# Retention feeding two MLPs: the first sweep's second token block runs inside the first block's sweep, with attention packed one chunk to a step

## The chip, the cores and the metric

One NeuronCore of a Trainium2 chip runs the whole kernel. The metric is the device time of one execution in microseconds (us), as the median of several runs. TensorE (PE) does the matmuls, VectorE (DVE), ScalarE (ACT) and GpSimd (POOL) do elementwise work, and SyncE (SP) issues most of the DMA transfers; ACT issues some too.

## The reference

```python
for t in range(768):            # 4 batches, 8 heads, head size 64
    state = gamma * state + k[t]^T v[t]
    y[t] = scale * q[t] @ state
x = y as 3072 tokens x 512
h = x @ w_in;  x = (h * cos(h)) @ w_out          # first MLP, 512 -> 2048 -> 512
h = x @ w_in2
g = h if h >= 1; 0 if h <= -1; else (h + 1)**2 / 4
out = g @ w_out2                                 # second MLP, same sizes
```

## The kernel before, in words

The retention is done by chunks of 128 positions: for chunk `n` PE makes the scores (`scores`, line 327), DVE multiplies them with a decay mask (`masks`, 339), PE adds scores times v and decayed q times the state (`attend`, 379 and 385), ACT and DVE split the result into a rounded part and a rest (`finish`, 117 and 399), PE makes k times v (`kv`, 350) and DVE puts it into the state of its batch (`update`, 365 and 367). POOL decays q and k (`decay_q` 315, `decay_k` 305). Chunk `n` belongs to position group `n // 4`; the state that chunk `n` reads is updated by chunk `n - 4`. Four chunks make one block of 512 tokens, so there are six blocks.

The first MLP has 16 slices of 128 hidden columns ("chunks" of the hidden size, `j`). A sweep `k = 0` runs all six blocks over the first eight, a sweep `k = 1` runs them over the other eight; the partial output of the first sweep is stored in `yp_d` and added in the second. A pair (block, slice) is a step. In step `i` PE does `first` (12 matmuls of 512 columns, line 435) and then `second` of step `i - 3` (12 matmuls, line 500), since activation and splitting of a step take that long. `act` puts the work of a step on ACT and DVE in a fixed order: h to integer part (448), product of the step before (476) and its rounding (477), remainder (452), absolute value (455), rest (480), sine (459), then the callbacks in `mid`, then the weight conversion. With the last slice of a block `evacuate` copies four PSUM banks out.

Weights come as 64-bit floats and have to be converted. A conversion passes through `Conveyor` in stages, one for each call of `advance`: load (SP, 143, into one of three `raw` buffers), one step later `one` (DVE, 150 and 154) and `two` (ACT, 159 and 160), then `three` (DVE, 165 and 169) and `four` (POOL, 175), then `five` (ACT rounds, 117: `wih` or `woh`) and `six` (POOL subtracts, 120: `wil` or `wol`). A matmul of slice `j` needs `wih`/`wil` for `first` and `woh`/`wol` three steps later. The first five conversions (w_in 0, 1, 2, w_out 0, w_in 3) are started ahead of step 0. Of the sweep's 16 weight tiles, 11 are left for steps 0 to 6.

Blocks come one after the other: steps 0 to 7 are block 0, 8 to 15 block 1. Ahead of step 0 stand the four chunks of block 0. The four chunks of the next block are spread over the eight steps of a block, scores in an even step and attend in the odd one. The order of each engine is the order in which the program writes it (a manual schedule); each engine runs its own list in order, and waits where an operand is not there yet.

Of the kernel before, what the change touches and what calls it, by code (L numbers as in the profile page):

```python
# [11 lines left out]
F32 = mybir.dt.float32  # L12
# [9 lines left out]
P = 128  # L22
# [18 lines left out]
def tile_retention_mlp_mlp(  # L41
# [21 lines left out]
    CB = TB // C  # L63
    LAG = 3
    NWARM = 10

# [3 lines left out]
    yT_d = [dram.tile([P, NP, TB], F32, name=f"yT{j}") for j in range(NB)]  # L70
    yp_d = [dram.tile([P, NP, TB], F32, name=f"yp{j}") for j in range(NB)]
    w32_d = {
        (m, j, a): dram.tile([P, TB], F32, name=f"w32_{m}_{j}_{a}")
# [178 lines left out]
    class Attention:  # L252
# [17 lines left out]
        def load_mask(self):  # L270
            nc.sync.dma_start(out=self.mask_sb, in_=mask.rearrange("p (r c t) -> p r c t", r=2, c=NP))

# [16 lines left out]
        def load_v(self, n):  # L289
            if n >= NCH:  # L290
                return
            self.v[n] = self.ap.tile([P, NP, P], F32, tag="v", name="v", bufs=5)
            nc.sync.dma_start(out=self.v[n], in_=v[n].rearrange("p (c s) -> p c s", c=NP))

# [112 lines left out]

    JS = (range(NH), range(NH, NF))
# [13 lines left out]
    def load_part(b):  # L422

        t = xt[1, b][0].bitcast(F32)
        nc.sync.dma_start(out=t, in_=yp_d[b])
        for e in range(NP):
            part[b, e] = t[:, e, :]

# [11 lines left out]

    def act(k, b, j, done=(), fill=(), mid=()):
# [25 lines left out]

# [17 lines left out]
    def second(i):  # L485
        k, b, j = steps[i]
        gh, gl = gs.pop((k, b, j))
        wh, wl = wt[0, j, 1]
        begin, last = j == JS[k][0], j == JS[k][-1]
        if begin:  # L490
            acc[k, b] = [bank(e) for e in range(NP)]
        parts = ((wh, gh), (wl, gh), (wh, gl))
        if last:
# [3 lines left out]
        for e, i in order:  # L497
            s = slice(e * P, (e + 1) * P)
            w, g = parts[i]
# [4 lines left out]
        return [(k, b, e) for e in range(NP)] if last else ()  # L504

    def evacuate(done, n):
        for k, b, e in itertools.islice(done, n):
            a = acc[k, b][e]
            o = tp.tile([P, TB], F32, tag="r", name="o", bufs=5)
            if e % 2 == 0 and k == 1:  # L510
                nc.vector.tensor_tensor(out=o, in0=a, in1=part.pop((b, e)), op=ALU.add)
            elif e % 2 == 0:
                nc.vector.tensor_copy(out=o, in_=a)
            else:
                nc.scalar.activation(out=o, in_=a, func=AF.Copy)
                if k == 1:
                    nc.gpsimd.tensor_tensor(out=o, in0=o, in1=part.pop((b, e)), op=ALU.add)
            nc.sync.dma_start(out=(yp_d, yT_d)[k][b][:, e, :], in_=o)

# [307 lines left out]
    def run():  # L827
        i = 0
        with ExitStack() as es:
            att = Attention(es)  # L830
            stage = es.enter_context(tc.tile_pool(name="stage", bufs=1, reuse_waits="tile"))

            order = sorted([(j + a * LAG, 1 - a, j, a) for j in range(NH) for a in range(2)])
            todo = [Convert(0, j, a, True) for _, _, j, a in order]
            todo += [Convert(0, j, a, False) for j in range(NH, NF) for a in range(2)]

            att.load_t(0)
            att.load_mask()
# [4 lines left out]
            att.load_t(2)  # L843
            att.load_v(2)
            att.load_t(3)
            att.load_v(3)

# [5 lines left out]

            att.scores(0, (4, 5))
            att.masks(0)
            att.scores(1, (6, 7))
            att.masks(1)
            for n in range(CB):
                att.attend(n, 2 + n % 2)
                att.finish(n)  # L860
                if n + 2 < CB:
                    att.scores(n + 2, (4, 5) if n % 2 == 0 else (6, 7))
                    att.masks(n + 2)
                if n != 2:
                    conv.step(todo.pop(0), stage)
                if n == 0:
                    att.load_kdec()
                    att.load_k(0)
                    att.load_t(CB)
            att.load_qdec(1)  # L870
            for n in range(1, CB):
                att.load_k(n)
            att.decay_k(0)
            conv.step(todo.pop(0), stage)
            att.load_v(CB)
            att.load_k(CB)
            att.load_t(CB + 1)
            att.decay_q(CB)
            for n in range(1, CB + 1):
                att.decay_k(n)  # L880
            count = iter((1, 1, 2, 2, 2, 2, 1))
            for b in range(NB - 1):
                for l in range(NH):
                    n = (b + 1) * CB + l // 2
                    now = next(count, 0) if b == 0 else (b == 1 or l % 2) and bool(todo)
                    conv.start(todo.pop(0) if now else None, stage)
                    first(*steps[i], 4 + i % 2)
                    if l % 2 == 0:
                        att.load_t(n + 2)
                        att.load_v(n + 1)  # L890
                        att.load_k(n + 1)
                        if l == 2:
                            att.load_qdec(b + 2)
                        att.scores(n, (6, 7))
                        mid = [lambda: att.masks(n)]
                        if i == 0:
                            att.kv(0, 0)
                            mid.append(lambda: att.update(0))
                    else:
                        att.decay_q(n + 1)  # L900
                        att.decay_k(n + 1)
                        att.attend(n, 7)
                        att.kv(n, 6)
                        mid = [lambda: att.finish(n), lambda: att.update(n)]
                        if i == 1:
                            for m in range(1, CB):
                                att.kv(m, m)
                                mid.append(lambda m=m: att.update(m))
                    done = second(i - LAG) if i >= LAG else ()
                    act(*steps[i], done, mid=mid)  # L910
                    if now == 2:
                        conv.step(todo.pop(0), stage)
                    i += 1
            assert not todo
# [3 lines left out]
        with ExitStack() as es:  # L918
# [6 lines left out]
            while i < len(steps):  # L925
                k, b, j = steps[i]
                l = j - JS[k][0]
                fill = []
# [3 lines left out]
                n = blocks.index((k, b)) + 1  # L932
                late = l - len(JS[k]) + NH
                if k == 1 and l == NH - 1:
# [13 lines left out]
                act(k, b, j, done, fill)  # L948
                if n < len(blocks) and late == LAG - 1:
                    load_parts(blocks[n][1])  # L950
# [76 lines left out]
```

## Time and profile before

| | |
|---|---|
| median of 3 runs | 1156.74 us (1156.09 to 1157.53) |
| the profiled execution | 1156.66 us |
| its span, first to last instruction | 1154.9 us |
| PE busy | 1122.9 us, 97% of the span |
| DVE, ACT, POOL busy | 781.2, 725.0, 470.1 us |
| granted TensorE clock, mean | 0.985 of full |

Some 1.8 us of the execution lie outside the span. A clock of 1.00 is 2.4 GHz; the lower level, 1.2 GHz, shows as 0.5. A matmul of 512 columns that follows another starts some 0.23 us after it at the higher level and some 0.43 us at the lower. PE's busy time counts slow matmuls as busy, so idle time and clock are read together.

### The profile page before, as it was taken

The numbers are of one execution on the slowest core, as the hardware profiler recorded it, in microseconds if no ns is written. First come the engines' busy times: TensorE is split into PE (matmuls) and PEld (weight loads), VectorE is DVE, ScalarE is ACT, GpSimd is POOL, SyncE is SP. The second block draws the span as 40 slices with busy tenths as digits, with TensorE's granted clock in tenths as the row PEclk, the third lists the DMA queues.
The fourth block names the chain that finished last, engine by engine and source line by source line (L and its number), as shares of the span: only waits on it lengthen the run. The fifth ranks groups of instructions, "written<-read, shape, count | busy, mean of one in ns | idle before, by whom it ended". The sixth has DMA issues, their size and how long they took to land.

```text
span 1154.9 us, 16558 instructions
## 1 busy us (share of the span) xinstructions
PE 1122.9 (97%) x5882; PEld 915.7 (79%) x5882; DVE 781.2 (68%) x1233; ACT 725.0 (63%) x1212; POOL 470.1 (41%) x402
## 2 busy tenths in 40 slices
PE   6689999999999999999999999999999999999998
PEld 4566888888888888888888878878888788888886
DVE  4898766565544467677776377677777677777776
ACT  2565654444436666667675587687768677676664
POOL 2664333221103333366663447564265572424320
PEclk7888999999999999999999999999999999999999
DMA  7736577544235176486573243549424468331211
GB/s 265 273 138 219 182 251 244 191 173 147 74 119 203 74 262 236 152 303 235 194 266 132 95 165 123 174 160 354 154 95 165 148 237 298 123 100 51 83 37 73
DMA packets 87026, 201.12 MB, mean 174 GB/s; under 512 B 9760, under 2 KB 14368, under 8 KB 83104
## 3 DMA queue, kind: packets, MB, share of 16 engines
q1 hardware_dynamic: 76000, 171.76, 42.5%
q10 hardware_dynamic: 10944, 28.32, 6.3%
q8 instruction: 46, 0.75, 0.3%
q14 instruction: 36, 0.29, 0.1%
HBM read 138.17 MB, written 61.87 MB: 173 GB/s over the span
## 4 chain that ended last, share of the span: by engine, by line
PE 83%; DVE 6%; ACT 6%; DMA 3%; issue 1%; SPq 0%; POOL 0%; DVEq 0%; ACTq 0%
PE b L500 22%; PE b L435 21%; PE b L682 18%; PE b L635 16%; PE b L327 2%; DMA wol<-w 2%; PE b L379 2%; PE b L385 1%; ACT r L650 1%; DVE b L664 1%; DVE cs L169 1%; ACT r L651 1%; ACT r L649 1%; DMA raw<-in_w 1%; ACT gh L665 1%
## 5 line engine op out<-in xcount | busy, mean ns | idle before, releaser
L120 POOL TENSOR_TENSOR wil<-wil,wih 128x512 fp32r<-128x512 f32 x108 | 124.5, 1182 | 258.4 <-ACT wih L117 249.3
L175 POOL TENSOR_TENSOR cf<-cf,cs 128x512 f32<-128x512 f32 x64 | 83.2, 1300 | 243.4 <-DVE cs L169 209.8
L452 DVE SCALAR_TENSOR_TENSOR r<-b,r 128x512 f32<-128x512 f32 x96 | 66.1, 689 | 169.0 <-ACT r L448 169.0
L435 PE MATMUL b<-xh,wih 128*128 128x512 f32 x384 | 153.8, 401 | 13.9 <-DVE pm L339 10.8
L448 ACT ACTIVATE r<-b 128x512 int32<-128x512 f32 x96 | 57.2, 595 | 169.6 <-PE b L435 164.3
L435 PE MATMUL b<-xh,wil 128*128 128x512 f32 x384 | 154.0, 401 | 3.6 <-POOL wil L120 3.6
L500 PE MATMUL b<-gh,woh 128*128 128x512 f32 x384 | 153.9, 401 | 0.0
L500 PE MATMUL b<-gh,wol 128*128 128x512 f32 x384 | 149.7, 390 | 0.0
L500 PE MATMUL b<-gl,woh 128*128 128x512 f32 x384 | 108.5, 389 | 0.0
L435 PE MATMUL b<-xl,wih 128*128 128x512 f32 x384 | 104.7, 395 | 0.0
L435 PEld LDWEIGHTS b<-xh,wih 128*128 128x128 f32 x384 | 74.1, 193 | 30.6 <-ACT wih L117 14.8
L721 DVE TENSOR_TENSOR b<-b,sum 128x512 f32<-128x512 f32 x120 | 83.4, 695 | 20.0 <-PE b L635 16.7
L435 PEld LDWEIGHTS b<-xh,wil 128*128 128x128 f32 x384 | 74.2, 193 | 21.3 <-POOL wil L120 5.9
L120 POOL TENSOR_TENSOR wol<-wol,woh 128x512 fp32r<-128x512 f32 x58 | 74.6, 1306 | 33.1 <-ACT woh L117 29.3
L649 ACT ACTIVATE r<-b,half 128x512 f32<-128x512 f32 x96 | 65.7, 684 | 33.9 <-DVE b L721 33.9
L500 PEld LDWEIGHTS b<-gh,woh 128*128 128x128 f32 x384 | 72.0, 188 | 18.0 <-issue 0.7
L435 PEld LDWEIGHTS b<-xl,wih 128*128 128x128 f32 x384 | 73.8, 192 | 15.8
L664 DVE TENSOR_TENSOR b<-b,r 128x512 f32<-128x512 f32 x96 | 67.0, 698 | 26.6 <-ACT r L651 18.8
L500 PEld LDWEIGHTS b<-gl,woh 128*128 128x128 f32 x384 | 72.1, 188 | 15.0
L500 PEld LDWEIGHTS b<-gh,wol 128*128 128x128 f32 x384 | 72.1, 188 | 13.9
L682 PE MATMUL b<-woh,woh 128*128 128x512 f32 x192 | 74.9, 390 | 0.4 <-DVE xl L695 0.4
L682 PE MATMUL b<-woh,gh 128*128 128x512 f32 x192 | 75.0, 390 | 0.3 <-ACT gh L665 0.3
(112 smaller groups left out, 2731.2 us busy)
## 6 DMA issues: line engine op xcount, KB each, us to landing
raw<-in_w SPq DMA_DIRECT2D x64, 512.0 KB, 5.0
wil<-wa SPq DMA_DIRECT2D x72, 256.0 KB, 3.4
wol<-w SPq DMA_DIRECT2D x56, 256.0 KB, 3.3
qk<-in_qk SPq DMA_DIRECT2D x23, 512.0 KB, 5.6
w<-cf ACTq DMA_DIRECT2D x32, 256.0 KB, 4.1
v<-in_v SPq DMA_DIRECT2D x24, 256.0 KB, 5.7
xTh<-xh ACTq DMA_DIRECT2D x6, 1024.0 KB, 3.9
xTl<-xl ACTq DMA_DIRECT2D x6, 1024.0 KB, 5.7
```

The lines of the kernel that those rows point to most:

```text
L120: nc.gpsimd.tensor_tensor(out=lo, in0=x, in1=hi.bitcast(F32), op=ALU.subtract)
L175: nc.gpsimd.tensor_tensor(out=self.f, in0=self.f, in1=self.s.bitcast(F32), op=ALU.mult)
L327: nc.tensor.matmul(out=s2[r][:, p, :], lhsT=t[o:o + D, 1, p, :], rhs=t[o:o + D, 0, p, :], start=True, stop=True,)
L435: nc.tensor.matmul(out=h, lhsT=w[:, c * P:(c + 1) * P], rhs=x[:, c, :], start=(i == 0), stop=(i == len(terms) - 1),)
L448: nc.scalar.activation(out=n, in_=h, func=AF.Identity, scale=INV_2PI)
L452: nc.vector.scalar_tensor_tensor(out=r, in0=h, scalar=INV_2PI, in1=n, op0=ALU.mult, op1=ALU.subtract)
L500: nc.tensor.matmul(out=acc[k, b][e], lhsT=w[:, s], rhs=g, start=(begin and i == 0), stop=(last and i == 2),)
L635: nc.tensor.matmul(out=to, lhsT=w[:, o:o + P], rhs=x, start=n == 0, stop=n == len(terms) - 1)
L649: nc.scalar.activation(out=r, in_=h, func=AF.Relu, scale=-0.5, bias=half)
L664: nc.vector.tensor_tensor(out=h, in0=h, in1=r, op=ALU.max)
L682: nc.tensor.matmul(out=y, lhsT=a[:, s], rhs=w, start=(i, m) == (0, 0), stop=(i, m) == (1, 2))
L721: nc.vector.tensor_tensor(out=o, in0=x, in1=y, op=ALU.add)
```

## The change: what it does

Block 1's eight steps are put inside block 0's: five steps of block 0 (slices 0 to 4), then all eight of block 1, then the last three of block 0 (slices 5 to 7). The order of the conversions follows: slices 5 to 7 of w_in and w_out come later, and there is one conversion a step up to step 11, with a second one in step 3. Block 0's partial output therefore leaves PSUM in two pieces, `yp_d[0]` after slice 4 and the new `yq_d` after slice 7; in sweep 1 block 0 adds both, so its four output tiles take four more additions on POOL, and 1 MB more is written and read back.

Block 1's four chunks have to be done by step 5, so a chunk takes one step: scores at the end of step `i`, attend in step `i + 1`, for steps 0 to 4; block 2's chunks do the same in steps 11 to 15. From step 16 on, two steps a chunk as before. In these dense steps the masks stand in `end`, behind the conversion, not in `mid`. Ahead of step 0 the four chunks use eight PSUM banks of their own pairs. The four state copies of block 0 go from DVE to ACT.

The first loads: mask and the four v tiles of block 0 are issued by ACT, and the q/k tiles and weights by SP; the sine's warm-up activation moves behind them. Further on, `qdec` and one `kd` load move ahead of the fourth weight load, and `v`, three `kd` and one q/k load move ahead of the fifth.

```diff
+    SPLIT = 5
-    nc.scalar.activation(out=const.tile([P, 1], F32, name="sine"), in_=half, func=AF.Sin)
-            nc.sync.dma_start(out=self.mask_sb, in_=mask.rearrange(...))
+            nc.scalar.dma_start(out=self.mask_sb, in_=mask.rearrange(...))
-            nc.sync.dma_start(out=self.v[n], ...)
+            (nc.scalar if n < CB else nc.sync).dma_start(out=self.v[n], ...)
-                    nc.vector.tensor_copy(out=s[h], in_=new)
+                    nc.scalar.activation(out=s[h], in_=new, func=AF.Copy)
-    steps = [(k, b, j) for k, b in blocks for j in JS[k]]
+    turns = [(0, 0, range(SPLIT)), (0, 1, range(NH)), (0, 0, range(SPLIT, NH))]
+    turns += [(0, b, range(NH)) for b in range(2, NB)]
+    turns += [(1, b, range(NH, NF)) for b in range(NB)]
+    steps = [(k, b, j) for k, b, js in turns for j in js]
         conv.advance()
+        for f in end:
+            f()
+        to = yT_d[b] if k else yq_d if (b, j) == (0, NH - 1) else yp_d[b]
...
+            for x in add:
+                nc.gpsimd.tensor_tensor(out=o, in0=o, in1=x, op=ALU.add)
...
-            order = sorted([(j + a * LAG, 1 - a, j, a) for j in range(NH) for a in range(2)])
+            order = sorted([
+                (j + (j >= SPLIT) * SPLIT + a * LAG, 1 - a, j, a) for j in range(NH) for a in range(2)
+            ])
...
+                if n < 3 * CB:
+                    i = 11 * (n // CB - 1) + c
+                    lead = (2, 1, 0) if n < 2 * CB else (3, 3, 0)
...
-                    now = next(count, 0) if b == 0 else (b == 1 or l % 2) and bool(todo)
+                now = (i < 12) + (i == 3) if i < 2 * NH else (i < 3 * NH or i % 2) and bool(todo)
```

DVE in step 0, from the remainder of step 0 on. `pm` is the masked score of chunk 4, `cs`/`cf` and `raw` belong to conversions. Before:

```order
L452 SCALAR_TENSOR_TENSOR r<-b_464,r 128x512 [waits Activation_49]
L339 TENSOR_TENSOR pm_507<-b_483,mask_sb 128x512 [waits PE_49]
L339 TENSOR_TENSOR pm_509<-b_484,mask_sb 128x512 [waits PE_49]
L365 COPY state_239<-b_493 64x4x64 [waits PE_49]
L365 COPY state_239<-b_493 64x4x64
L150 TENSOR_SCALAR cs<-raw 128x512 [waits DMAHW7_49,Pool_49]
L154 TENSOR_SCALAR cf<-raw 128x512 [waits Pool_49]
L165 SCALAR_TENSOR_TENSOR cf<-raw,cf 128x512
L169 SCALAR_TENSOR_TENSOR cs<-raw,cs 128x512
```

The same place with the change:

```order
L456 SCALAR_TENSOR_TENSOR r<-b_465,r 128x512 [waits Activation_49]
L149 TENSOR_SCALAR cs<-raw 128x512 [waits DMAHW2_49,Pool_49]
L153 TENSOR_SCALAR cf<-raw 128x512 [waits Pool_49]
L164 SCALAR_TENSOR_TENSOR cf<-raw,cf 128x512
L168 SCALAR_TENSOR_TENSOR cs<-raw,cs 128x512
L338 TENSOR_TENSOR pm_523<-b_493,mask_sb 128x512 [waits PE_49]
L338 TENSOR_TENSOR pm_525<-b_494,mask_sb 128x512 [waits PE_49]
```

The masks of chunk 4 stood ahead of the conversion that waits for the fifth weight load (w_in 3); now they stand behind it.

SP, from the fourth weight load (w_out 0) to the sixth; `DMAHW` are the completion semaphores of eight earlier transfers, taken in turn. Before:

```order
L143 DMA raw_411<-in_w1 128x1024 [waits DMAHW0_49,DVE_49]
L278 DMA qdec_426<-in_qdec 128x512 [waits DMAHW2_49]
L300 DMA kd_428<-in_kn 128x512 [waits DMAHW3_49]
L300 DMA kd_430<-in_kn 128x512 [waits DMAHW4_49]
L300 DMA kd_432<-in_kn 128x512 [waits DMAHW6_49]
L143 DMA raw_435<-in_w1 128x1024 [waits DMAHW7_49,DVE_49]
L293 DMA v_450<-in_v 128x512 [waits DMAHW0_49]
L300 DMA kd_452<-in_kn 128x512 [waits DMAHW1_49]
L287 DMA qk_454<-in_qk 128x1024 [waits DMAHW2_49,PE_49]
L143 DMA raw_462<-in_w1 128x1024 [waits DMAHW3_49,DVE_49]
```

The same place with the change:

```order
L277 DMA qdec_412<-in_qdec 128x512 [waits DMAHW0_49]
L299 DMA kd_414<-in_kn 128x512 [waits DMAHW1_49]
L142 DMA raw_416<-in_w1 128x1024 [waits DMAHW2_49,DVE_49]
L292 DMA v_431<-in_v 128x512 [waits DMAHW4_49]
L299 DMA kd_433<-in_kn 128x512 [waits DMAHW5_49]
L299 DMA kd_435<-in_kn 128x512 [waits DMAHW6_49]
L299 DMA kd_437<-in_kn 128x512 [waits DMAHW0_49]
L286 DMA qk_439<-in_qk 128x1024 [waits DMAHW1_49,PE_49]
L142 DMA raw_442<-in_w1 128x1024 [waits DMAHW3_49,DMAHW2_49,DVE_49]
L142 DMA raw_463<-in_w1 128x1024 [waits DMAHW7_49,DMAHW3_49,DVE_49]
```

Two loads of 256 KB left the stretch between the fourth and the fifth weight load upwards, v, `kd` of chunk 4 and q/k of chunk 5 (1 MB) came into it from below; the fifth weight load (`raw_442`) now also waits until the fourth has landed.

## Rows read from the trace of the kernel before

**Rows 1.** The page: PE's busy tenths in 40 slices of the span

```profile
PE   6689999999999999999999999999999999999998
```

**Rows 2.** Windows by stage: length, busy time by engine, clock, DMA share, GB/s

```profile
0.00:25.08 25.08, 16.45 (x139) 11.39 (x139) 11.53 (x22) 6.89 (x12) 3.52 (x13) 0.83 0.73 255
25.08:107.14 82.06, 64.98 (x476) 49.66 (x477) 69.28 (x102) 45.53 (x74) 50.80 (x41) 0.84 0.58 211
107.14:166.29 59.15, 59.15 (x449) 48.48 (x448) 43.22 (x75) 33.10 (x54) 21.95 (x18) 1.00 0.59 207
```

**Rows 3.** PE timeline: start, length, work, idle ahead and releaser

```profile
32.07 0.69 PE L350 MATMUL b<-v,kd 128*64 128x64 f32 x16
...
37.66 0.44 PE L385 MATMUL b<-pm,v 128*64 128x128 f32 x4 [1.59 <-DMA v<-in_v]
...
53.04 0.79 PE L435 MATMUL b<-xh,wih 128*128 128x512 f32 x1 [6.43 <-DVE pm L339]
...
74.20 0.50 PE L435 MATMUL b<-xh,wih 128*128 128x512 f32 x1 [2.27 <-DVE pm L339]
75.68 0.79 PE L435 MATMUL b<-xh,wil 128*128 128x512 f32 x1 [0.98 <-POOL wil L120]
...
86.30 0.39 PE L435 MATMUL b<-xh,wih 128*128 128x512 f32 x1
```

**Rows 4.** PE timeline, steps 9 and 11: first matmul of each

```profile
113.90 0.39 PE L435 MATMUL b<-xh,wih 128*128 128x512 f32 x1
...
128.69 0.39 PE L435 MATMUL b<-xh,wih 128*128 128x512 f32 x1
```

**Rows 5.** ACT timeline, two steps of sweep 1 without attention

```profile
437.26 0.60 ACT L448 ACTIVATE r<-b 128x512 int32<-128x512 f32 x1 [2.69 <-PE b L435]
...
442.70 0.60 ACT L448 ACTIVATE r<-b 128x512 int32<-128x512 f32 x1 [1.47 <-PE b L435]
```

**Rows 6.** SP's queue, two rows of 13 to 28 us

```profile
13.68 9.03 SPq L143 DMA_DIRECT2D raw<-in_w  x2
...
26.97 0.33 SPq L143 DMA_DIRECT2D raw<-in_w  x1
```

**Rows 7.** DVE timeline: conversions and chain of steps 0 and 3

```profile
37.05 0.92 DVE L150 TENSOR_SCALAR cs<-raw 128x512 int32<-128x512 int32 x1 [2.41 <-DMA raw<-in_w]
...
38.84 1.53 DVE L169 SCALAR_TENSOR_TENSOR cs<-raw,cs 128x512 int32<-128x512 int32 x1
...
45.13 2.60 DVE L365 COPY state<-b 64x256 f32<-64x256 f32 x6
...
59.94 0.68 DVE L476 TENSOR_TENSOR b<-b,r 128x512 f32<-128x512 f32 x1
...
64.64 0.64 DVE L150 TENSOR_SCALAR cs<-raw 128x512 int32<-128x512 int32 x1
...
66.74 0.41 DVE L150 TENSOR_SCALAR cs<-raw 128x512 int32<-128x512 int32 x1
...
70.92 0.70 DVE L476 TENSOR_TENSOR b<-b,r 128x512 f32<-128x512 f32 x1
...
72.89 1.28 DVE L339 TENSOR_TENSOR pm<-b,mask_sb 128x512 f32<-128x512 f32 x2
```

**Rows 8.** Windows of the same form: loads behind the start, and a wait's end

```profile
25.08:32.69 7.61, 7.04 (x45) 5.13 (x45) 6.68 (x8) 3.73 (x6) 5.73 (x5) 0.65 0.98 378
...
53.04:58.71 5.67, 4.98 (x13) 3.34 (x13) 5.67 (x8) 2.69 (x5) 3.34 (x3) 0.59 0.86 320
```

**Rows 9.** Groups of 25 to 107 us: POOL's product, ACT's rounding

```profile
L175 POOL TENSOR_TENSOR cf<-cf,cs 128x512 f32<-128x512 f32 x13 | 17.1, 1318 | 16.4 <-DVE cs L169 16.4
...
L117 ACT ACTIVATE wih<-cf 128x512 fp32r<-128x512 f32 x8 | 5.0, 620 | 3.3 <-POOL cf L175 2.1 <-DVE cs L150 1.2
```

**Rows 10.** ACT timeline where block 0 is evacuated

```profile
127.53 0.60 ACT L515 ACTIVATE o<-b 128x512 f32<-128x512 f32 x1 [0.69 <-PE b L500]
```

**Rows 11.** POOL timeline where sweep 1 adds block 0's partial output

```profile
445.26 2.73 POOL L517 TENSOR_TENSOR o<-o,xh 128x512 f32<-128x512 f32 x2 [5.90 <-DVE o L511]
```

More of the change, by code (lines that the diff above doesn't have):

```diff
@@ L422, in load_part @@
     def load_part(b):
[L424 to L427, printed above, removed]
+        for t, d in zip(xt[1, b], (yp_d[b], yq_d)[:1 + (b == 0)]):
+            t = t.bitcast(F32)
+            nc.sync.dma_start(out=t, in_=d)
+            for e in range(NP):
+                part.setdefault((b, e), []).append(t[:, e, :])
     def first(k, b, j, hbank):
@@ L503, in second @@
             )
-        return [(k, b, e) for e in range(NP)] if last else ()
+        return [(k, b, e, to) for e in range(NP)] if last else ()
     def evacuate(done, n):
[L507 to L511, printed above, removed]
+        for k, b, e, to in itertools.islice(done, n):
+            a, o = acc[k, b][e], tp.tile([P, TB], F32, tag="r", name="o", bufs=5)
+            add = part.pop((b, e)) if k else []
+            if e % 2 == 0 and add:
+                nc.vector.tensor_tensor(out=o, in0=a, in1=add.pop(0), op=ALU.add)
             elif e % 2 == 0:
@@ L842, in run @@
             conv.start(todo.pop(0), stage)
[L843 to L846, printed above, removed]
+            for n in range(2, CB):
+                att.load_t(n)
+                att.load_v(n)
+            nc.scalar.activation(out=const.tile([P, 1], F32, name="sine"), in_=half, func=AF.Sin)
             warm = const.tile([P, TB], BF16, name="warm")
@@ L852, in run @@
                 nc.tensor.matmul(out=b0, lhsT=warm[:, :P], rhs=warm, start=True, stop=True)
[L854 to L859, printed above, removed]
-                att.finish(n)
[L861 to L866, printed above, removed]
+            at = ((4, 5), (6, 7), (0, 1), (2, 3))
+            for n in range(2):
+                att.scores(n, at[n])
+                att.masks(n)
+            for n in range(2):
+                att.attend(n, at[n][0])
+                att.finish(n)
+                att.scores(n + 2, at[n + 2])
+                att.masks(n + 2)
+                if n:
                     att.load_kdec()
@@ L869, in run @@
                     att.load_t(CB)
+                convert()
+            for n in range(2, CB):
+                att.attend(n, at[n][0])
+                att.finish(n)
             att.load_qdec(1)
-            for n in range(1, CB):
+            att.load_k(1)
+            convert()
+            att.load_v(CB)
+            for n in range(2, CB + 1):
                 att.load_k(n)
+            att.load_t(CB + 1)
             att.decay_k(0)
[L874 to L877, printed above, removed]
+            convert()
             att.decay_q(CB)
@@ L880, in run @@
                 att.decay_k(n)
[L881 to L884, printed above, removed]
-                    now = next(count, 0) if b == 0 else (b == 1 or l % 2) and bool(todo)
[L886 to L913, printed above, removed]
@@ new lines, in run @@
+            place = {1: (2, 3), 2: (0, 2)}
+            for i in range(NH * (NB - 1)):
+                load_t, load_v, decay, early, late, attend = plan[i]
+                now = (i < 12) + (i == 3) if i < 2 * NH else (i < 3 * NH or i % 2) and bool(todo)
+                conv.start(todo.pop(0) if now else None, stage)
+                first(*steps[i], 4 + i % 2)
+                for n in load_t:
+                    att.load_t(n)
+                for n in load_v:
+                    att.load_v(n)
+                    att.load_k(n)
+                if i % NH == 5:
+                    att.load_qdec(i // NH + 2)
+                for n in decay:
+                    att.decay_q(n)
+                    att.decay_k(n)
+                mid, end = [], []
+                for n in attend:
+                    by, bk = place.get(i, (7, 6))
+                    att.attend(n, by)
+                    att.kv(n, bk)
+                    mid += [lambda n=n: att.finish(n), lambda n=n: att.update(n)]
+                for n in early:
+                    att.scores(n, (6, 7))
+                    mid.append(lambda n=n: att.masks(n))
+                done = second(i - LAG) if i >= LAG else ()
+                for m, bk in ((0, 0),) if i == 0 else ((1, 1),) if i == 1 else ((2, 3), (3, 1)) if i == 2 else ():
+                    att.kv(m, bk)
+                    end.append(lambda m=m: att.update(m))
+                for n in late:
+                    att.scores(n, (6, 7))
+                    end.append(lambda n=n: att.masks(n))
+                act(*steps[i], done, mid=mid, end=end)
+                if now == 2:
+                    convert()
@@ L914, in run @@
+            i += 1
             assert not todo
@@ L948, in run @@
                 act(k, b, j, done, fill)
-                if n < len(blocks) and late == LAG - 1:
+                if n < len(blocks) and l == LAG - 1:
                     load_parts(blocks[n][1])
```

37 lines of the change are left out of this document (24 added, 13 removed).

## The prediction

> **What bounds the kernel now.** I read the page's slices first. PE is busy in nine tenths or more of nearly every slice; only the first three, some 87 us, and the last fall below [rows 1]. So a change of order can win only near the start. The windows by stage size it [rows 2]. From the first matmul of step 0 (25.08 us) to that of step 8 (107.14) pass 82.06 us, in which PE has 64.98 us of work at a mean clock of 0.84. From step 8 to step 16 (166.29) PE never stops, at full clock, in 59.15 us.
>
> How much of the 82.06 is lost follows from the price of a step. Two steps of sweep 1 without attention start 5.44 us apart [rows 5]; steps 9 and 11, with one chunk of attention between them, 14.79 us [rows 4], so a chunk costs PE 14.79 - 2 x 5.44 = 3.91 us. Check: eight steps and four chunks are 8 x 5.44 + 4 x 3.91 = 59.2 us, as the window says. Steps 0 to 7 hold the same, less three `second` passes (3 x 2.72 = 8.2 us), plus four `kv` of block 0 at about 0.6 us [rows 3]: 53.4 us. Hence 28.7 us are lost there, and that is the most this change could win.
>
> What PE waits for stands in its timeline: 6.43 us ahead of step 3, 2.27 and 0.98 ahead of step 5 [rows 3]. The releaser named is DVE's mask for two of them, but a `first` needs no mask: the matmul at 53.04 reads `wih` of a fresh slice, the one at 75.68 `wil`. DVE is the engine that feeds these weights, with 69.28 busy us of 82.06 [rows 2]. After such a wait the clock is low as well: 0.59 from 53.04 to 58.71 [rows 8], so mostly 1.2 GHz after an idle 6.43 us.
>
> **The change part by part.** *Steps 5 to 9* now reuse slices 0 to 4, so no weight can be late there, and slices 5 to 7 are wanted at steps 10 to 12, with conversions started in steps 4 to 6 and ready three steps later. PE should run them at 5.44 us. *Steps 0 to 4* hold all of block 1's attention: the wait moves there, and I follow it.
>
> Attend of chunk 4 (call its start A4; A5 to A7 are the later ones) needs its masks, and these now stand behind a conversion whose `one` waits for the fifth weight load. In the trace that load was issued at 26.97 [rows 6], and DVE sat 2.41 us until 37.05 for it [rows 7]. Now it has 1.5 MB of SP's loads between it and the fourth, where it had 1.0; 0.5 MB at 378 GB/s [rows 8] are 1.3 us. It also waits until the fourth has landed. Against that, two loads leave their place behind the 9.03 us stall on a `raw` buffer [rows 6] and move in a gap. Bounds 35.5 and 39.5; I take 37.7, near the row. The conversion's DVE part took from 37.05 to 40.37 there (38.84 + 1.53), 3.3 us, and two masks 1.28 [rows 7]: **A4 = 42.3**. In the trace PE resumed chunk 4's attend at 37.66, held only by v [rows 3]; so step 1 gets later, not earlier.
>
> A4 to A5. PE has one chunk (3.91), one more `kv` (0.6) and a `first` (2.72): 7.2 us at full clock. But it has idled over 6 us, and in the 5.67 us after 53.04 the clock was 0.59 [rows 8], which cost 0.41 x 5.67 = 2.3 us: 9.5 us, while DVE would want 8.1 (below). I take **9.3**.
>
> A5 to A6. Here DVE sets the pace. In step 3 the row at 59.94 starts the chain, and its first conversion ended when the second began, 66.74 [rows 7]: 6.8 us for product, remainder, rest, `finish`, `update` and one conversion, 2.1 of them the conversion (64.64 to 66.74). With 1.28 of masks **8.1**; PE's own work is 7.8 with the two `kv` there and is hidden.
>
> A6 to step 4's first matmul. `wih` of slice 4 is converted in step 3: DVE 6.8, POOL's product 1.32, ACT's rounding 0.62 [rows 9]: **8.7**. PE's share (a chunk and a `second`, 6.6) ends 2.1 us earlier, a wait like the 2.27 of the trace.
>
> Step 4 to step 5. The same sequence stands in the trace at step 5: wait for `wih`, wait for `wil`, slow clock, attend, `kv`, `second`, from 74.20 to 86.30 [rows 3]: **12.1**.
>
> So step 5 starts at 42.3 + 9.3 + 8.1 + 8.7 + 12.1 = 80.5 us. Steps 5 to 10: 6 x 5.44 = 32.6. Steps 11 to 15: 5 x 5.44 + 4 x 3.91 = 42.8; their conversions run out, and DVE's loop of 8.1 us less the conversion is 6.0, under PE's 9.35 for such a step, so no wait. One exception: in step 15 block 1 is evacuated while ACT must still deliver chunk 11. ACT's copy of bank 1 waits for half of `second` (1.36 us); in the trace it also waited 0.69 us for PE and took 0.60 [rows 10]. With sine and rounding at about 0.6 each behind it, some 3.3 us against `second`'s 2.72: 0.6 us of wait. Step 16 then starts at 156.5, against 166.29: **9.8 us earlier**.
>
> *Costed at nothing:* the second piece of block 0's partial output. Two copies each on DVE and ACT in step 18 lie in steps where PE has the larger share; 1 MB out and 1 MB in move under a DMA share of 0.59 [rows 2]. The four additions on POOL are 4 x 1.37 us, beside two that took 2.73 after an idle 5.90 [rows 11]; without that cover they delay output tiles by 5.5 us, which is one step, and the buffers are wanted again after that, so at most 2 us. *The state copies on ACT:* eight copies that took DVE 0.43 us each (six in 2.60) [rows 7], an estimate of 3.5 us for ACT, which was busy 45.53 of 82.06 us [rows 2]; the one for chunk 4 stands behind the same weight load as the masks and is ready with them. *The first loads on two queues:* step 0 is worth little now, since A4 hangs on the fifth weight load; bounds plus or minus 1 us, taken as 0.
>
> Sum: the profiled execution took 1156.66 us (0.08 under the median), less 9.8: **1146.9 us**. All links at their lower bounds (load at 35.5, conversion 2.1, A5 8.1 later, step 4 without the clock's 2.3 and the 0.98) give step 5 at 73 and a total of 1139; all at the upper ones (load at 39.5, conversions of 4.2 as from 66.74 to 70.92 [rows 7]) give step 5 at 88 and a total of 1155.
>
> **The rivals.** *Stretched conversions, 1152.* DVE's conversion took 2.1 us at 64.64 but 4.2 at 66.74 [rows 7], and an instruction at 38.84 took 1.53. If in the dense steps, where POOL also has two decays per chunk, every conversion is of the long kind, the three links from A4 to step 4 that hold one grow by 2.1 us where DVE sets them: some 5 us, 1152. For it: POOL was already busy 50.80 of 82.06 us [rows 2]. Against it: the decays fall early in the step, the conversion late. The Trainium skill's page "SBUF — State Buffer", section "SBUF: two separate sides", says that DVE and GpSimd lock a common pair of ports for a whole instruction and that the other engine blocks. By that rule the long kind is DVE behind a POOL operation, and the same 1152 follows if each conversion meets two of them; the trace agrees as to the 1.53.
>
> *The weights come in time, 1138.* If the masks of A4 hardly wait, because the fifth load lands with the fourth (28 us), A4 is near 35; PE then hardly idles, the clock stays up, and the links are 7.5, 8.1, 8.7 and 10: step 5 at some 70 to 72, total 1138. Against it: 10 us from issue to landing in the trace.
>
> *The clock stays low, slower, 1167.* A wait precedes each attend and step 4. From A4 to step 5 PE has four chunks less the first scores, three `kv`, three `first` and two `second`, about 30 us at 2.4 GHz, within the 38.2 us that I give it. If it runs wholly at 1.2 GHz that is 60 us; the waits vanish in it, but for some 4 us on weights: step 5 at 106 and a total of 1172, and with four fifths of it so, 1167. It turns the result to slower once about half of that work runs at 1.2 GHz (30 + 15 + 4 = 49 us, against 38.2 + 9.8), that is a mean clock under about 0.7 in that stretch. For it: after waits of 6.43 and 2.27 us the matmuls were slow [rows 3]. Against it: from 25 to 107 us, with as many waits, the mean was 0.84 [rows 2]. The Trainium skill's "TensorE: Matmul & The Clock Gate", section "What's actually happening", has the half rate as the idle state and activity as what lifts it, which speaks against packing waits together; by it the time is this rival's only if no busy stretch comes between, and a mean of 0.84 cannot come about without such stretches.
>
> *No gain, 1155.* The wait only moves: all links at the upper bounds.
>
> **How the numbers follow.** The forecast gets 0.58, with 1143 to 1150 as its own range; stretched conversions 0.17; weights in time 0.12; low clock 0.07; no gain 0.06. The range for 8 in 10 reaches from 1139 to 1154: about half of the early case lies under it, low clock and no gain over it. A change within 0.2% (2.3 us, about what measuring can tell) takes the no-gain case and a little of the stretched one, 0.07; slower 0.08; faster 0.85.
>
> **What would show it.** After the change PE should wait some 6 us ahead of chunk 4's attend, with DVE's `one` released by a weight load near 37 to 38 us; attends some 8 to 9.5 us apart; a wait of about 2 us ahead of step 4 on `wih`; no wait at all from step 5 (near 80 us) on, at clock 1.00; step 16 near 156 us, and everything after it as before. It is wrong if that load lands much earlier or later, if PE's clock stays under 0.7 up to 80 us, or if steps 5 to 15 show waits, on weights or on attention.

## The result, and the profile after

| | before | after |
|---|---|---|
| median of 4 runs each, us | 1157.12 | 1143.85 (1143.57 to 1146.24) |
| ratio, 95% interval | | 0.9891 [0.9874, 0.9908] |
| the profiled execution / its span | 1156.66 / 1154.9 | 1143.57 / 1141.8 |
| start of step 0 | 25.08 | 24.25 |
| start of step 16 (block 2's first) | 166.29 | 156.32 |
| from there to the last instruction | 988.61 | 985.48 |

The change is faster by 1.1%, 1143.85 us against a forecast of 1146.9. Step 16 starts 9.97 us earlier, where 9.8 were forecast. The rest, 3.13 us, comes from a stretch that was to stay as it was; that is taken up below.

PE's slices in the page of the changed kernel answer to [rows 1]:

```profile
PE   7789999999999999999999999999999999999998
```

The first two slices went from 6 to 7 tenths. No more shows at this scale, so the stages have to be windowed. The windows of the changed kernel, in the columns of [rows 2] (start:end, length, busy time with instruction counts of PE, weight load, DVE, ACT and POOL, clock, DMA share, GB/s), are cut at step 0, the attends of chunks 4, 5 and 6 (A4, A5, A6), steps 4 and 5, near step 11, and step 16:

```profile
24.25:40.69 16.44, 10.12 (x56) 7.39 (x57) 10.35 (x12) 7.45 (x13) 13.11 (x11) 0.81 0.93 365
40.69:50.89 10.20, 10.20 (x93) 8.76 (x93) 8.04 (x16) 5.89 (x11) 6.03 (x6) 0.70 0.46 161
50.89:59.37 8.48, 7.68 (x109) 6.39 (x109) 6.92 (x13) 6.35 (x13) 4.92 (x6) 1.00 0.40 137
59.37:68.22 8.85, 6.51 (x76) 5.44 (x76) 7.46 (x15) 5.42 (x10) 4.70 (x4) 1.00 0.22 77
68.22:79.40 11.18, 9.98 (x72) 7.81 (x73) 5.85 (x9) 4.73 (x8) 2.90 (x2) 0.85 0.28 109
79.40:112.00 32.60, 32.60 (x144) 26.67 (x144) 26.14 (x45) 25.30 (x43) 16.85 (x12) 1.00 0.73 255
112.00:156.32 44.32, 43.48 (x379) 35.11 (x377) 28.58 (x48) 20.68 (x35) 22.08 (x18) 1.00 0.34 119
156.32:1141.80 985.48, 980.44 (x4820) 806.92 (x4820) 668.07 (x1056) 645.12 (x1082) 402.82 (x337) 1.00 0.49 175
```

Three stretches lie under full clock, each with a wait at its head: from step 0, from A4 and from step 4. From step 5 on PE is at 1.00 and, up to step 11, busy all the time. The PE timeline names the waits (compare [rows 3]):

```profile
24.25 0.80 PE L439 MATMUL b<-xh,wih 128*128 128x512 f32 x1 [2.58 <-ACT wih L116]
...
40.69 1.00 PE L378 MATMUL b<-qd,state 128*64 128x128 f32 x4 [5.75 <-ACT state L364]
...
59.37 0.44 PE L378 MATMUL b<-qd,state 128*64 128x128 f32 x4 [0.44 <-DVE pm L338]
...
68.22 0.50 PE L439 MATMUL b<-xh,wih 128*128 128x512 f32 x1 [2.34 <-ACT wih L116]
69.92 0.50 PE L439 MATMUL b<-xh,wil 128*128 128x512 f32 x1 [1.20 <-POOL wil L119]
...
122.44 0.44 PE L378 MATMUL b<-qd,state 128*64 128x128 f32 x4 [0.42 <-DVE pm L338]
...
156.32 0.50 PE L439 MATMUL b<-xh,wih 128*128 128x512 f32 x1 [0.42 <-ACT xh L116]
```

The one ahead of A4 hangs on DVE's list, as its timeline shows (compare [rows 7]): DVE idles 5.29 us until the fifth weight load lands, converts, and reaches the masks at 40.65. Further down, a conversion in a dense step takes from 47.38 to 49.58:

```profile
37.11 1.00 DVE L149 TENSOR_SCALAR cs<-raw 128x512 int32<-128x512 int32 x1 [5.29 <-DMA raw<-in_w]
38.04 1.48 DVE L153 TENSOR_SCALAR cf<-raw 128x512 int32<-128x512 int32 x1
...
40.65 1.27 DVE L338 TENSOR_TENSOR pm<-b,mask_sb 128x512 f32<-128x512 f32 x2
...
47.38 0.63 DVE L149 TENSOR_SCALAR cs<-raw 128x512 int32<-128x512 int32 x1
...
49.58 1.29 DVE L338 TENSOR_TENSOR pm<-b,mask_sb 128x512 f32<-128x512 f32 x2
```

### The profile page after: what moved, and what is told of

Same layout as the page of the kernel before. It is cut to its first block, busy times and chain, and to the rows that moved or that the text cites. A ratio compares the mean times of both kernels' runs of the same rounds, so it can differ in the third digit from the quotient of the medians.

```text
span 1141.8 us, 16576 instructions
## 1 busy us (share of the span) xinstructions
PE 1117.3 (98%) x5882; PEld 915.7 (80%) x5882; DVE 772.9 (68%) x1227; ACT 727.8 (64%) x1222; POOL 476.9 (42%) x406
## 3 DMA queue, kind: packets, MB, share of 16 engines
q1 hardware_dynamic: 76000, 172.28, 43.2%
## 4 chain that ended last, share of the span: by engine, by line
PE 89%; ACT 4%; DMA 3%; DVE 3%; issue 1%; POOL 0%; SPq 0%; DVEq 0%; ACTq 0%
PE b L507 22%; PE b L439 22%; PE b L689 21%; PE b L642 18%; PE b L378 2%; PE b L326 2%; PE b L384 2%; DMA raw<-in_w 1%; ACT r L657 1%; PE b L349 1%; DVE b L671 1%; DMA wol<-w 1%; ACT r L658 1%; DMA qk<-in_qk 1%; ACT r L656 1%
## 5 line engine op out<-in xcount | busy, mean ns | idle before, releaser
L439 PE MATMUL b<-xh,wil 128*128 128x512 f32 x384 | 151.4, 394 | 2.1 <-POOL wil L119 2.1
L459 ACT ACTIVATE r<-r 128x512 f32<-128x512 f32 x96 | 60.8, 633 | 22.7 <-DVE r L456 22.6
```

Source lines behind the costliest of these rows:

```text
L439: nc.tensor.matmul(out=h, lhsT=w[:, c * P:(c + 1) * P], rhs=x[:, c, :], start=(i == 0), stop=(i == len(terms) - 1),)
```

## The experiments

All times are in us; a ratio is to the kernel before, measured beside the variant on the same chip. Since the intervals of neighbouring variants overlap, the table also gives the links read from each one's PE timeline, in one profiled execution: starts of step 0, A4, step 4 and step 16. Step 0 itself starts anywhere from 23.80 to 25.63, and in the five profiles with the changed kernel's order on DVE from step 0 to A4 (after, k0, e1, e6, e7) A4 follows it by 16.42 to 16.45 us, so the start of step 0 is passed on in full. What an edit behind step 0 does is therefore read from step 0 on; the sixth column gives that for step 16 (141.21 in the kernel before).

| run | step 0 | A4 | step 4 | step 16 | step 0 to 16 | median | ratio, interval |
|---|---|---|---|---|---|---|---|
| after | 24.25 | 40.69 | 68.22 | 156.32 | 132.07 | 1143.85 | 0.9891 [0.9874, 0.9908] |
| k0, changed kernel again | 24.21 | 40.64 | 67.43 | 156.47 | 132.26 | 1144.35 | 0.9906 [0.9889, 0.9922] |
| e1, old first loads | 25.53 | 41.98 | 68.91 | 158.00 | 132.47 | 1145.82 | 0.9913 [0.9898, 0.9928] |
| e2, late store | 24.54 | 36.22 | 66.06 | 155.04 | 130.50 | 1143.00 | 0.9885 [0.9867, 0.9903] |
| e3, masks first | 25.63 | 36.84 | 67.95 | 156.00 | 130.37 | 1143.41 | 0.9895 [0.9878, 0.9913] |
| e4, not nested | 24.84 | 40.10 | 67.84 | 164.58 | 139.74 | 1153.66 | 0.9972 [0.9962, 0.9982] |
| e5, state copies on DVE | 24.25 | 41.21 | 71.50 | 160.32 | 136.07 | 1147.89 | 0.9931 [0.9913, 0.9950] |
| e6, fill | 23.92 | 40.37 | 66.84 | 154.78 | 130.86 | 1143.44 | 0.9881 [0.9867, 0.9895] |
| e7, w_in 4 first | 25.39 | 41.81 | 66.65 | 152.79 | 127.40 | 1140.64 | 0.9855 [0.9840, 0.9870] |
| e8, late store, masks first | 24.49 | 35.29 | 65.88 | 153.92 | 129.43 | 1142.30 | 0.9870 [0.9856, 0.9884] |
| e9, late store, w_in 4 first | 23.80 | 35.47 | 62.73 | 148.84 | 125.04 | 1137.64 | 0.9838 [0.9817, 0.9858] |
| e10, all three | 24.87 | 36.17 | 64.60 | 150.72 | 125.85 | 1137.77 | 0.9839 [0.9818, 0.9861] |

**The changed kernel again.** 

> The changed kernel once more, nothing edited. Its first profile reached step 16 at 156.32 us, 9.97 earlier than before, and took 985.48 us from there to the end, against 988.61 before: 3.13 us that the change should not have touched. Theory: those 3.1 us are landing times of weight loads in the second MLP, which vary from run to run; this profile should again reach step 16 within 0.3 us of 156.3, while its rest may lie anywhere from 985 to 989 us. Rival: the change shifts the second MLP in a fixed way; then the rest is again 985.5 within 0.3 us.

The links up to A4 repeat within 0.05 us and step 16 within 0.15; A5 (50.89 and 49.58) and step 4 do not. Their two readings are below, under what was not expected. The rest takes 985.93 us, 0.45 more than at first: that lies in the theory's range, and so near the rival's 0.3 us that it does not rule out a fixed shift.

**First loads in the old order.** The lines of the diff that touch mask, v and sine are undone.

> The changed kernel with the first loads as before: mask and v of block 0 from SP, the sine's activation first. Theory (attend of chunk 4 hangs on the landing of the fifth weight load, not on the start of step 0): step 0 starts 0.8 us later, at about 25.1, and step 16 within 1 us of 156.3; total 1143 to 1146. Rival (an earlier start is passed on in full, or the two queues also speed the later loads): step 16 later by 0.8 us or more than 2 us, total above 1146.

Step 0 starts at 25.53, 1.3 us later, and step 16 1.5 to 1.7 us later; the median rises by 1.5 against k0, measured beside it, with intervals that overlap. The prediction held this part worthless since A4 hangs on the fifth weight load. That load lands later too, at 38.35 instead of 37.11: the reason was wrong. Over all profiles here step 0 starts at 25.08 to 25.53 with the old loads (three) and at 23.80 to 25.63 with the new (eleven, mean 24.6), so this part may be worth some 0.8 us. That is less than single profiles differ, and two of the eleven start as late as with the old loads (e3, e7): the gain is not shown.

**The store of x behind step 5.** ACT issues 2 MB of stores ahead of step 0 in the changed kernel:

```diff
-            if o == CB - 1:
+            if o == CB - 1 and j:
...
+                if i == 5:
+                    att.store(0)
```

> The changed kernel with the 2 MB store of block 0's x moved from ahead of step 0 to behind step 5, so that it does not share the transfers with the fifth weight load. Theory (the load lands at 37.1 us because 2 MB of stores and 1.5 MB of loads go out with it): it lands at 32 to 34, attend of chunk 4 starts at 36 to 37.5 instead of 40.69, and PE has idled too little to lose its clock; step 16 some 4 to 6 us earlier, total 1138 to 1140. Rival (the load is late because it is issued at 26.9 and is itself slow, or the next link, DVE's, takes over): attend of chunk 4 earlier by under 1.5 us, total within 1.5 us of the changed kernel.

A4 comes at 36.22, 4.5 us earlier, but step 4 only 1.4 to 2.2, and step 16 1.3 (from step 0 on 1.6 to 1.8). The time, 1143.00, is where the rival has it and not the theory, and its interval overlaps those of the changed kernel. Three weight loads issued between 20 and 40 us took a median of 7.1 us to land in the changed kernel and four took 4.2 here, and DVE no longer waits for the fifth. But its timeline shows the conversion that follows:

```profile
32.48 1.14 DVE L149 TENSOR_SCALAR cs<-raw 128x512 int32<-128x512 int32 x1
33.54 1.51 DVE L153 TENSOR_SCALAR cf<-raw 128x512 int32<-128x512 int32 x1
34.97 1.53 DVE L164 SCALAR_TENSOR_TENSOR cf<-raw,cf 128x512 f32<-128x512 uint32 x1
36.42 1.52 DVE L168 SCALAR_TENSOR_TENSOR cs<-raw,cs 128x512 int32<-128x512 int32 x1
37.87 1.27 DVE L338 TENSOR_TENSOR pm<-b,mask_sb 128x512 f32<-128x512 f32 x2
```

It takes 5.39 us, against 3.5 in the changed kernel and 2.2 in its later steps, and PE waits a second time, 1.64 us at 38.60, for `pm`. The windows of this stretch, in the columns above, show POOL busy without a gap:

```profile
32.48:37.87 5.39, 3.03 (x15) 1.92 (x13) 5.39 (x6) 4.43 (x8) 5.39 (x5) 1.00 0.82 291
```

So the earlier load is partly paid for by a conversion that now falls together with POOL's decays; POOL's four decays of k lengthen too, to 5.12 us from 4.05 in the changed kernel. The masks behind the conversion, which read PSUM, are not stretched, though the decays go on until 39.8.

**The masks of chunk 4 ahead of step 0's conversion.**

```diff
+                if i == 0:
+                    att.kv(0, 0)
+                    mid.append(lambda: att.update(0))
+                    att.scores(CB, (6, 7))
+                    mid.append(lambda: att.masks(CB))
+                    late.remove(CB)
...
```

> The changed kernel with the masks of chunk 4 and the state copy of chunk 0 put ahead of step 0's conversion, on DVE and ACT, as the masks stood before the change. Theory (the new wait is one of order, the masks queued behind a load they do not need): attend of chunk 4 starts near 35 to 36 us, right behind step 1's first, but the conversion still waits until 37.1 and the masks of chunk 5 stand behind the next one, so attend of chunk 5 moves by less, to 46 to 48 instead of 50.89; step 16 3 to 5 us earlier, total 1139 to 1141. Rival (DVE's loop from the load on sets the pace, whatever the masks do): step 16 within 1 us, total 1143 to 1145.

A4 comes at 36.84 without a wait, but the waits reappear: 2.63 us ahead of step 2's `first` (released by `gl`, the rest of step 0's product, from DVE) and 2.01 ahead of A5. Step 4 and step 16 come only 0.3 us earlier than at first, as the rival says. But step 0 came 1.4 us later in this profile, and the fifth load with it, at 38.48. From step 0 on, step 4 comes after 42.3 us, against 44.0 and 43.2 in the two profiles of the changed kernel: 0.9 to 1.7 us less, about the 1.28 us of the masks, which no longer stand in DVE's list behind the load. The medians do not separate that. So the place of the masks made little of the wait; most of it is DVE, which goes through the rest of its list from the landing of the load on.

**Blocks one after the other, attention still packed.** `SPLIT = 8`, and the conversions of block 0 as before (1, 1, 2, 2, 2, 2, 1, 0 in its steps, then one each in steps 8 and 9); nothing of the rest is undone. So this takes back the nesting and the later conversions that it allows, together.

> Blocks 0 and 1 one after the other again, as before; attention stays packed one chunk a step in steps 0 to 4 and 11 to 15, and the new first loads, the bank pairs and the state copies on ScalarE stay. Sixteen weight tiles are therefore needed within block 0 once more. Theory (the nesting gains, because the changed kernel never needs two conversions in a step but once): steps 2 to 5 now carry two conversions (4.2 us on DVE in the profile of the changed kernel) beside masks, products and state, so that each takes 9 to 11 us instead of 8.5 and the weights of slices 4 to 7 come late; block 2's pass starts at 160 to 166 instead of 156.3 and the time is 1148 to 1155. Rival (packing the attention and the first loads gain, nesting adds nothing): block 2's pass starts within 1.5 us of 156.3, and the time is 1143 to 1146.

The theory's numbers are met: step 4 at 67.84, as nested, but step 16 at 164.58, 8.3 us later (7.7 to 8.6 from step 4 on, against the two profiles of the changed kernel), and 1153.66. The PE timeline shows the waits that nesting removes, on the weights of slices 5, 6 and 7:

```profile
78.04 0.50 PE L439 MATMUL b<-xh,wih 128*128 128x512 f32 x1 [1.84 <-ACT wih L116]
79.39 0.79 PE L439 MATMUL b<-xh,wil 128*128 128x512 f32 x1 [0.84 <-POOL wil L119]
...
88.20 0.50 PE L439 MATMUL b<-xh,wih 128*128 128x512 f32 x1 [1.91 <-ACT wih L116]
90.02 0.79 PE L439 MATMUL b<-xh,wil 128*128 128x512 f32 x1 [1.32 <-POOL wil L119]
...
100.08 0.50 PE L439 MATMUL b<-xh,wil 128*128 128x512 f32 x1 [1.15 <-POOL wil L119]
```

They add to 7.06 us, and PE runs slowly behind some of them (a clock of 0.68 from 78.04 to 83.40).

**State copies back on DVE.** `nc.vector.tensor_copy` in `update`.

> The four state copies of block 0 go back to DVE; all else as changed. Theory (DVE's list sets steps 0 to 3): each copy of some 0.85 us stands in the list ahead of masks; A4 comes 0.5 to 1 us later, at 41.2 to 41.7, block 2's pass at 157 to 158 instead of 156.3, and the time rises by 0.7 to 1.5 us. Rival (DVE waits 1.3 to 2.0 us a step for ScalarE's rounded x, and the copies fit in there): block 2's pass within 0.4 us of 156.3, the time within 0.5 us.

Neither: step 16 comes 4.0 us later and the time is 1147.89. DVE's timeline shows why. The rows 46.82 and 55.83 are the same place of two steps, 9.01 us apart; in the changed kernel they stand at 45.89 and 54.25, 8.36 apart. The next step, to 65.76, holds two chunks' copies and takes 9.93 us, against 8.23:

```profile
46.82 0.69 DVE L398 TENSOR_TENSOR xl<-b,xh 128x512 fp32r<-128x512 f32 x1 [2.01 <-ACT xh L116]
...
50.50 0.87 DVE L364 COPY state<-b 64x256 f32<-64x256 f32 x2
...
55.83 0.69 DVE L398 TENSOR_TENSOR xl<-b,xh 128x512 fp32r<-128x512 f32 x1 [1.17 <-ACT xh L116]
...
59.53 1.78 DVE L364 COPY state<-b 64x256 f32<-64x256 f32 x4
...
65.76 0.69 DVE L398 TENSOR_TENSOR xl<-b,xh 128x512 fp32r<-128x512 f32 x1 [1.17 <-ACT xh L116]
```

The idle time ahead of each such row is a wait for ACT's `xh`, the rounded part of the attention's result, which itself follows PE's attend, and that follows DVE's masks: it is part of the loop and hides nothing. Four chunks' copies at 0.87 us make 3.5 us; step 4 comes 3.3 us later (4.1 against k0).

**Fill for the wait ahead of A4.** 22 matmuls on constant data in step 1, into a free bank.

> 22 extra matmuls on constant data (into a PSUM bank that is free then; the output is unchanged) run ahead of the attend of chunk 4, where PE otherwise waits 5.75 us and the granted clock falls. They take some 5 us at the higher level. Theory (the low clock behind the wait costs time of its own): chunk 4's attend, k times v and the start of step 2 run at the higher level, A4 to A5 falls from 10.2 to about 8.3 us, and the time falls by 1.3 to 2.0 us. Rival (the loop over DVE, 8.1 to 8.5 us a step, or the second weight of slice 4 sets the pace behind it): a new wait of 1 to 2 us stands ahead of A5 or step 4, and the time falls by less than 0.6 us.

The PE timeline has the fill (21 of its matmuls are recorded) and the attends of chunks 4 and 5:

```profile
35.23 4.70 PE L937 MATMUL b<-warm 128*128 128x512 bf16 x21
40.37 0.74 PE L379 MATMUL b<-qd,state 128*64 128x128 f32 x4 [0.44 <-ACT state L365]
...
48.65 0.74 PE L379 MATMUL b<-qd,state 128*64 128x128 f32 x4 [0.28 <-ACT state L365]
```

A4 to A5 falls from 10.20 to 8.28 us, at clock 1.00, as the theory says; but k0, without the fill, took 8.94 us there at clock 0.81, so the clock behind the wait costs 0.7 to 1.9 us. A5 to A6 grows to 9.34, from 8.48 and 9.00 in k0, so that 0.3 to 1.1 us remain by A6, and step 16 comes 1.2 to 1.4 us earlier from step 0 on. In the medians that is not separated from the changed kernel (0.9881 against 0.9891 and 0.9906).

**w_in of slice 4 ahead of w_out of slice 1.**

```diff
+            todo[5:7] = todo[6:4:-1]
```

> Conversions of w_out of slice 1 and of w_in of slice 4 change places, so that slice 4's w_in is loaded and converted a step earlier and slice 1's w_out a step later. In the changed kernel PE waits 2.34 us ahead of step 4 for the rounded w_in of slice 4 and 1.20 us for its rest. Theory (the order of two conversions alone makes that wait): both waits go, slice 1's w_out is ready by the time that step 4's second half needs it (2.8 us and an attend later), block 2's pass starts 2.5 to 3.5 us earlier at about 153.3, and the time falls by 2.5 to 3.5 us to about 1141. Rival (DVE sets the pace of steps 1 to 4, the wait moves): the waits appear ahead of A7 or of step 4's second half with 2 us or more, and the time falls by less than 1 us.

The wait ahead of step 4 is gone, and nothing took its place but 0.76 us ahead of step 5:

```profile
66.65 0.50 PE L439 MATMUL b<-xh,wih 128*128 128x512 f32 x1
...
81.19 0.51 PE L439 MATMUL b<-xh,wih 128*128 128x512 f32 x1 [0.76 <-DVE gl L486]
...
152.79 0.51 PE L439 MATMUL b<-xh,wih 128*128 128x512 f32 x1 [0.42 <-ACT xh L116]
```

Step 16 comes 3.5 us earlier although step 0 was 1.1 later here, 4.7 to 4.9 from step 0 on, and the interval of the median lies below both of the changed kernel's. Of the two waits of 3.54 us and the slow matmuls behind them, A6 to step 16 gives back 4.4 us (96.95 to 92.54). The order of the conversions, not the amount of DVE's work, made this wait.

**Late store and masks first.** 

> Both earlier edits: the 2 MB store of block 0's x moved behind step 5, and the masks of chunk 4 ahead of step 0's conversion. The store's move alone brought A4 from 40.6 to 36.2 but left 1.64 us of wait for the mask product behind it; the masks' move alone brought A4 to 36.8 but DVE, held by the late load, gave it back by A5. Theory (DVE's list from the landing of the fifth load on sets steps 1 to 3): together A4 comes at 35 to 36 without a second wait, but A5 comes no earlier than with the store's move alone (47.9), step 4 at 65.5 to 66.5, and the time is within 0.7 us of that of the store's move alone. Rival (the two waits add): step 4 comes 1.5 us or more earlier than 66.06, and the time falls by 1.5 us more.

Step 4 at 65.88 and step 16 at 153.92, against 66.06 and 155.04; the median 0.7 us under e2's, with intervals that overlap. Up to step 4 the theory held: the two edits together gain hardly more than the store's alone. Most of the difference at step 16 arises behind step 4, where e2 took 88.98 us and this kernel 88.04, by the clock at its head (below).

**Late store and w_in 4 first.** 

> The late store of block 0's x and slice 4's w_in ahead of slice 1's w_out, together. Theory (they cure two waits one behind the other, ahead of A4 and ahead of step 4, so they add): 1.3 us of the one and 3.5 us of the other, block 2's pass at 151.2 to 151.8 and the time 1139 to 1140.5. Rival (with both gone, DVE's list is the bound and takes back the smaller): block 2's pass at 152.3 or later, as with the order of conversions alone.

Step 16 at 148.84, 7.5 us before the changed kernel's, and 1137.64, the lowest median here, against 1139 to 1140.5 in the theory. From step 0 on it is 7.0 us, where the two edits gave 1.6 and 4.7 by themselves: the sum and little more. The theory's sum was smaller because it took e7's gain as 3.5 us, without its late step 0. Against e2, 0.74 of the 6.2 us lies ahead of step 0, and A6 to step 16 takes 92.51 instead of 97.84: e2 had the slower clock behind step 4, and here there is no wait that it could follow.

**All three.** 

> The late store, the masks of chunk 4 ahead of step 0's conversion, and slice 4's w_in ahead of slice 1's w_out. Theory (they add, since the first two brought block 2's pass to 153.9 and the third is worth 3.5 us): block 2's pass at 150.2 to 150.8, the time 1137.5 to 1139.5. Rival (DVE's list takes 8.2 us a step from its first conversion on, and gives back what comes earlier than that): block 2's pass no earlier than with the late store and the order of conversions (151.2 to 151.8).

Step 16 at 150.72 and 1137.77. These are the theory's numbers, but not for its reason, since e9 came out earlier than reckoned: from step 0 to step 4 this kernel takes 39.73 us and e9 38.93, and the medians are equal. The masks' move adds nothing once the store is late, as the rival says.

**The kernel before, profiled again.** 

> The kernel before, unchanged, profiled a second time. From the start of block 2's pass to the last instruction it took 988.6 us in its first profile, and the kernel changed takes 985.5; the six other variants so far took 984.7 to 987.3, all with the same instructions from there on but for the four added tiles. Theory (the landing of weight loads in the second MLP varies from run to run): the stretch comes out between 984.5 and 987.5 this time. Rival (the change itself shortens the second MLP): 988.0 to 989.2 again.

Step 16 starts at 166.68, and the stretch from there takes 987.12:

```profile
166.68:1153.80 987.12, 981.32 (x4821) 806.59 (x4819) 656.07 (x1038) 638.97 (x1073) 393.69 (x331) 1.00 0.48 167
```

The eleven nested kernels take 984.70 to 987.30 there, with a mean of 986.0. The theory's range holds, so part of the 3.13 us is what one profile differs from the next. But the two profiles of before lie 2.6 and 1.1 us above that mean, and the medians of `before` and `after` differ by 13.3 us (11.1 in k0's runs), of which some 10 lie ahead of step 16: 1 to 3 us may be the change's. Nor is the stretch the same work: besides the four additions, 46 of the first-stage conversions on DVE fall into it in the changed kernel and 42 before. What shortens it stays open, and that landing times make its spread is not shown.

## Why the prediction was right

**The mechanism.** The loss was weights that come late in the first pass, and nesting lets five slices serve eight more steps before the next are wanted: from step 5 to step 11 PE does not wait at all. e4 isolates this part, with the later conversions that belong to it: some 8 us of the 9.97 up to step 16, all of it behind step 4. An earlier step 0 gives 0.8 of the rest (25.08 to 24.25), which the sum had at nothing; that it comes from the new first loads is not shown. The state copies on ACT, which were costed at nothing there, save 3.3 us or more up to step 4 that packed attention would otherwise lose; DVE's loop of 8.1 us was reckoned without them, so the sum had it right.

**The links.** A4 was forecast at 42.3 and came at 40.69: the fifth load landed at 37.11 (37.7 forecast), the conversion took 3.5 us (3.3 reckoned), and the attend starts on the first state copy, while the masks still run. A4 to A5: 10.20 against 9.3, with the clock at 0.70 over the whole stretch, which is 3.1 us (0.30 x 10.20) where 2.3 were taken; in k0 it was 8.94 at 0.81, 1.7 us. A5 to A6 8.48 (k0 9.00) against 8.1, A6 to step 4 8.85 in both against 8.7. The prediction has these two set by DVE's own list, but its 6.8 us from the trace of before held a wait that it did not name:

```profile
63.15 0.69 DVE L399 TENSOR_TENSOR xl<-b,xh 128x512 fp32r<-128x512 f32 x1 [1.18 <-ACT xh L117]
```

It had the length of the loop over PE and ACT that e5 shows, taken for work of DVE. Step 4 to 5: 11.2 against 12.1, because the attend at 74.24 ran at the higher level again (12.2 in k0, where it did not at once). Step 5 then starts at 79.46 against 80.5; steps 5 to 15 take 76.86 against 76.0, among it an unforeseen 0.42 us on the masks of chunk 8 at 122.44, a wait of the kind that the prediction named as a sign of being wrong, but a small one; the wait ahead of step 16 was 0.42 against 0.6. The deviations cancel to 0.2 us, so the closeness at step 16 is partly luck. The remaining distance to 1143.85 is the last stretch, whose size in one profile was taken for fixed; what shortened it stays open.

**The rivals.** Stretched conversions: not in the links that the rival names, whose three conversions take 2.2 us each (the one ahead of A4 took 3.5 and the second of step 3 3.0). e2 shows the mechanism itself when a conversion falls beside POOL: each of four instructions at 1.14 to 1.53 us, 5.39 together. The Trainium skill's "SBUF — State Buffer", section "SBUF: two separate sides", has DVE and GpSimd exclude each other for a whole instruction, and e2's rows agree (1.51 us where 0.42 is usual). Weights in time: not so, the wait was 5.75 us; e2 comes near its A4 (36.22) but not its 1138, which only e9 and e10 reach, with the conversions exchanged as well. Low clock: 0.88 from A4 to step 5, above the rival's bound of 0.7. e6 shows that the clock behind the wait did cost 0.7 to 1.9 us of the next link, part of which came back as a longer link behind it.

## What to carry to other kernels

Where an instruction that waits for a load stands in an in-order list, ask what loops through that list: here moving the masks out of its way gained about their own length (0.9 to 1.7 us up to step 4) and nothing once the store was late, moving 2 MB of stores out of the load's way 1.7 to 2.5 us up to step 4, neither of them separated in the medians; exchanging two conversions so that the one wanted first is made first gained 4.7 us up to step 16 and, with the late store, 7.0. Profiles are compared from a common point: step 0 started up to 1.8 us apart, which hides or feigns a gain of that size. An engine's idle time covers extra work only if it is not itself a link of the loop that sets the pace; DVE's 1.2 to 2.0 us a step did not cover copies of 0.87. A small move to another engine can be what lets a big reordering pay.

## What was not expected of the hardware

The same program, with the same wait ahead, ran the same twelve matmuls of step 4 at different clocks. The windows from step 4 to the attend of chunk 7, first in the repeated run of the changed kernel, then in its first profile:

```profile
67.43:74.13 6.70, 5.49 (x12) 3.65 (x13) 2.81 (x3) 1.17 (x2) 2.91 (x2) 0.54 0.30 112
```

```profile
68.22:74.24 6.02, 4.82 (x12) 3.18 (x12) 2.81 (x3) 1.18 (x2) 2.90 (x2) 0.72 0.35 128
```

At 0.54 and 0.72, that is nearly all and about half of it at 1.2 GHz, after waits of 2.37 and 2.34 us. From A4 to A5 it went the other way, 0.70 at first and 0.81 in the repeated run, after waits of 5.75 and 5.40 us:

```profile
40.64:49.58 8.94, 8.94 (x93) 7.53 (x93) 7.28 (x14) 5.90 (x11) 5.26 (x5) 0.81 0.53 178
```

From step 4 to step 16 the runs with this wait fall into two groups, 87.9 to 88.1 us (after, e3, e6, e8; 0.71 to 0.72 from step 4 to A7) and 88.8 to 89.1 (k0, e1, e2, e5; 0.51 to 0.55): differences of about 1 us behind a wait are no evidence between variants. What decides between the two was not settled.
